# Four 64x64 tiles in place of a block-diagonal product for P V, a half batch in one step

## The chip, the cores and the metric

The kernel runs on one NeuronCore of one Trainium2 chip. The metric is the device time of one execution in microseconds (us); lower is better. The profiler records every instruction of TensorE (PE, with its weight loads as PEld), VectorE (DVE), ScalarE (ACT), GpSimd (POOL) and of the DMA queues.

## The reference

Linformer attention, then a gated feed-forward block. All inputs and the output are float32; the kernel works in bfloat16 with float32 accumulation.

```python
batch, n_heads, seq, head_dim, k_proj = 8, 8, 1024, 64, 64
k_proj = np.einsum('ks,bhsd->bhkd', E, k)
v_proj = np.einsum('ks,bhsd->bhkd', F, v)
scores = scale * np.matmul(q, k_proj.transpose(0, 1, 3, 2))
attn = softmax(scores)                       # over the 64 projected keys
attn_out = np.matmul(attn, v_proj)           # "P V": (1024 x 64) @ (64 x 64) for each head
x = attn_out.transpose(0, 2, 1, 3).reshape(8192, 512)
g = x @ w_gate; val = x @ w_val              # 512 -> 1536
return (g * sigmoid(g) * val) @ w_out        # 1536 -> 512
```

## The kernel before

**Chunks and steps.** A batch has two halves of 512 tokens; a half batch is a *chunk*, `c = 2*b + ch`, 0 to 15. The feed-forward block is the main loop: chunk `c` has 12 steps `f`, and a step `t = 12*c + f` computes one tile of 128 hidden features. `f_g` runs four 128x512 matmuls into a PSUM bank of pool `g` (two banks) and a tanh on ACT (line 474). `f_v` runs four more into a bank of pool `v` (two banks), and DVE joins them with two operations: line 481 (`s`, needs the tanh) and line 486 (`hT`, needs `s` and the `v` bank).

**Down projection.** Of chunk `c - 1`, it runs inside chunk `c`, from `late[t]`, right after `f_v` of its step. It is a seven-product scheme over two halves `p` of the token tiles: `f_m(c, n)`, `n` from 0 to 13, with `p, n % 7` choosing the product `m` in the order 3, 4, 5, 2, 1, 6, 7. A product is six 128x256 matmuls (line 564). Products 3, 4, 5, 2 of a half share the bank `y` (one bank); 1, 6, 7 share the bank `z` (one bank), and product 7 accumulates onto the columns that product 1 has filled. Between them, after product 6, `m_16` reads product 1 out of bank `z` on DVE (line 593), then adds on POOL (line 594). After product 7, `m_7` finishes on DVE (line 599) and the result is stored.

**Attention of later batches.** It is threaded through the main loop by slots: `slots[2*t]` runs between `f_g` and `f_v` of step `t`, and `slots[2*t + 1]` after `late[t]`. `place(b)` chooses the slots: the K and V projections (`u_KV`: 16 matmuls, 128x64 stationary, which write K to PSUM partitions 0 to 63 and V to 64 to 127 of one bank), scores and exp (`u_S`, eight a batch), row sums (`u_R` on DVE), normalisation (`u_N` on POOL), a transposing DMA (`u_AD`) that leaves the probabilities in `AT` with a pair of heads on the 128 partitions, and P V (`u_PV`).

**P V.** For a pair of heads, `BDV` holds the two projected 64x64 V matrices on the diagonal of a 128x128 tile, zeros elsewhere. One `u_PV` is one 128x512 matmul (line 410) into a bank of pool `a` (two banks), and one ACT copy (line 150) into `xT`, the input of the feed-forward block. A chunk needs four. In batches 3 to 7 the four of the first half are at slots 39, 41, 43, 45 from the batch's `s0 = 48*(b-1)`, which is after `f_v` of steps 7 to 10 of the odd chunk `2b - 1`; those of the second half at 57 to 63, steps 4 to 7 of the even chunk `2b`.

Nothing is reordered: every engine runs its instructions in the order in which this code issues them, and the banks come from rings (`bank`).

Of the kernel before, what the change touches and what calls it, by code (L numbers as in the profile page):

```python
# [18 lines left out]
D = 64  # L19
# [3 lines left out]
P = 128  # L23
# [15 lines left out]
def kernel(  # L39
# [38 lines left out]
    ident_bf = const.tile([P, P], BF16, name="ident_bf")  # L78
    ident_fp = fw.tile([P, P], FP32, name="ident_fp", tag="th")
    BD = [const.tile([P, H, P], BF16, name=f"BD{i}") for i in range(2)]  # L80
    BDV = [const.tile([P, NPAIR, P], BF16, name=f"BDV{i}") for i in range(2)]
    ks = [const.tile([P, H, D], BF16, name=f"ks{i}") for i in range(2)]
    ksp = [const.tile([P, NPAIR, D], BF16, name=f"ksp{i}") for i in range(2)]
    ET = const.tile([P, NJ, KP], BF16, name="ET")
# [67 lines left out]
    def u_KV(b, what="kv", hs=(0, H), at="a"):  # L152

        key = (b, what)
        if key not in kvp:
            kvp[key] = bank(at, [P, H, D], FP32, "kvp")
        t = kvp[key]
        h0, h1 = hs
        todo = [x for x in (("k", 0, ET, kb), ("v", 64, FT, vb)) if x[0] in what]
        for j in range(NJ):  # L160
            for _, lo, w, src in todo:
                nc.tensor.matmul(  # L162
                    out=t[lo : lo + 64, h0:h1].rearrange("p h d -> p (h d)"),
                    lhsT=w[:, j, :],
                    rhs=src[b][:, h0:h1, j, :],
                    start=(j == 0),
                    stop=(j == NJ - 1),
                )
        if "k" in what:
            nc.scalar.copy(out=ks[b % 2][0:64, h0:h1], in_=t[0:64, h0:h1])  # L170
        if "v" in what:
            tv = t[64:128].rearrange("p (a c) d -> p a c d", c=2)
            ps = slice(h0 // 2, h1 // 2)
            nc.vector.tensor_copy(out=BDV[b % 2][0:64, ps, 0:64], in_=tv[:, ps, 0, :])
            nc.vector.tensor_copy(out=BDV[b % 2][64:128, ps, 64:128], in_=tv[:, ps, 1, :])
        if h1 == H:
            kvp.pop(key)

# [15 lines left out]

    def u_V1(b, at="a"):

        t = bank(at, [P, NPAIR, D], FP32, "kvp")
        src = vb[b][:].rearrange("p (a c) j d -> p a c j d", c=2)
        for j in range(NJ):
            for c in range(2):  # L200
                nc.tensor.matmul(
                    out=t[64 * c : 64 * c + 64],
                    lhsT=FT[:, j, :],
                    rhs=src[:, :, c, j, :],
                    start=(j == 0),
                    stop=(j == NJ - 1),
                )
        for c in range(2):
            rows = slice(64 * c, 64 * c + 64)
            nc.vector.tensor_copy(out=BDV[b % 2][rows, :, rows], in_=t[rows])  # L210

    def u_V0(p0, p1, at):

        t = bank(at, [P, p1 - p0, P], FP32, "kvp")
        nc.tensor.matmul(
            out=t[:].rearrange("p a d -> p (a d)"),
            lhsT=zeros[:, 0:P], rhs=zeros[:, 0 : (p1 - p0) * P],
            start=True, stop=False,
        )
        src = vb[0][:].rearrange("p (a c) j d -> p a c j d", c=2)  # L220
        for j in range(NJ):
            for c in range(2):
                nc.tensor.matmul(
                    out=t[64 * c : 64 * c + 64, :, 64 * c : 64 * c + 64],
                    lhsT=FT[:, j, :],
                    rhs=src[:, p0:p1, c, j, :],
                    start=False,
                    stop=(j == NJ - 1),
                )
        nc.scalar.copy(out=BDV[0][:, p0:p1, :], in_=t[:])  # L230

    def u_V0w(p0, p1, at):

        t = bank(at, [P, p1 - p0, 2, D], FP32, "kvp")
        for j in range(NJ):
            nc.tensor.matmul(
                out=t[64:P].rearrange("p a c d -> p (a c) d"),
                lhsT=FT[:, j, :],
                rhs=vb[0][:, 2 * p0 : 2 * p1, j, :],
                start=(j == 0),  # L240
                stop=(j == NJ - 1),
            )
        for c in range(2):
            rows = slice(64 * c, 64 * c + 64)
            nc.scalar.copy(out=BDV[0][rows, p0:p1, rows], in_=t[64:P, :, c, :])

    def turn_ksp(t, b, g):
        nc.tensor.matmul(
# [95 lines left out]
    def u_S(b, u, at="a"):  # L344
        ch, w = divmod(u, 4)
        g, i = divmod(w, 2)
        ps = bank(at, [P, 4, P], FP32, "sc")
        if (b, ch) in BY_DMA:
            t = qT[b, ch, "d"][:].rearrange("p (h i) t -> p i h t", i=2)[:, i, 4 * g : 4 * g + 4]
        else:  # L350
            t = qT.pop((b, u))
        for n in range(4):
            nc.tensor.matmul(  # L353
                out=ps[:, n, :], lhsT=t[:, n, :], rhs=BD[b % 2][:, 4 * g + n, :], start=True, stop=True
            )
        e = aw.tile([P, 4, 2, KP], FP32, name="ee", tag="ee", bufs=4)
        nc.scalar.activation(  # L357
            out=e[:].rearrange("p h j k -> p (h j k)"),
            in_=ps[:].rearrange("p a k -> p (a k)"),
            func=AF.Exp,  # L360
            scale=scale,
        )
        ee[b, u] = e
# [42 lines left out]
    def u_PV(b, ch, pr, eng=nc.scalar):  # L406
        if (b, ch) not in xT:
            xT[b, ch] = x_pool.tile([P, NPAIR, CW], BF16, name="xT", tag=f"xT{ch}")
        ps = bank("a", [P, CW], FP32, "pv")
        nc.tensor.matmul(  # L410
            out=ps[:].rearrange("p (j t) -> p j t", t=P),
            lhsT=BDV[b % 2][:, pr, :],
            rhs=AT[b, ch][:, :, pr, :],
            start=True,
            stop=True,
        )
        copy(eng, xT[b, ch][:, pr, :], ps[:])

    def u_PV2(b, ch, g, i, eng):

        if (b, ch) not in xT:
            xT[b, ch] = x_pool.tile([P, NPAIR, CW], BF16, name="xT", tag=f"xT{ch}")
        ps = bank("a", [P, 2, CW // 2], FP32, "pv")
        for n in range(2):
            nc.tensor.matmul(
                out=ps[:, n].rearrange("p (j t) -> p j t", t=P),
                lhsT=BDV[b % 2][:, 2 * g + n, :],
                rhs=AT[b, ch][:, 2 * i : 2 * i + 2, 2 * g + n, :],
                start=True,
                stop=True,  # L430
            )
        copy(eng, xT[b, ch][:, 2 * g : 2 * g + 2, 256 * i : 256 * (i + 1)], ps[:])

    def u_PV1(b, ch, pr, i, eng):

        ps = bank("a", [P, CW // 2], FP32, "pv")
        nc.tensor.matmul(
            out=ps[:].rearrange("p (j t) -> p j t", t=P),
            lhsT=BDV[b % 2][:, pr, :],
            rhs=AT[b, ch][:, 2 * i : 2 * i + 2, pr, :],  # L440
            start=True,
            stop=True,
        )
        copy(eng, xT[b, ch][:, pr, 256 * i : 256 * (i + 1)], ps[:])
# [211 lines left out]
    def put(s, fn, *a):  # L656
        slots[s].append((fn, a))

    def place(b):
        s0 = 48 * (b - 1)  # L660
        if b == 1:
            put(22, u_TD, 1, 0)
            put(29, u_K1, 1)
            put(32, u_KT, 1)
            put(40, u_V1, 1)
            sa = (35, 36, 37, 38, 41, 42, 43, 44)
            put(41, u_AD, 1, 0)
            put(30, u_TD, 1, 1)
            put(47, u_AD, 1, 1)
            sp = (44, 45, 46, 46, 66, 67, 68, 69)  # L670
        else:
            put(s0 + (10 if b == 2 else 0), u_KV, b)
            put(s0 + (13 if b == 2 else 3), u_KT, b)
            o = 17 if b == 2 else 6
            put(s0 + (9 if b == 2 else -6), u_TD, b, 0)
            put(s0 + (11 if b == 2 else -4), u_TD, b, 1)
            sa = [s0 + o + 3 * j for j in range(NJ)]
            put(sa[3] + 4, u_AD, b, 0)
            put(sa[7] + 4, u_AD, b, 1)
            sp = [s0 + i for i in ((41, 43, 45, 46) if b == 2 else (39, 41, 43, 45)) + (57, 59, 61, 63)]  # L680
        for j in range(NJ):
            put(sa[j], u_S, b, j)
            put(sa[j] + 1, u_R, b, j)
            put(sa[j] + 1, u_N, b, j)
        for i in range(8):
            put(sp[i], u_PV, b, i // 4, i % 4)

    def run_slot(s):
        for fn, a in slots.pop(s, ()):
# [2 lines left out]
    with tc.manual_schedule():  # L692
# [17 lines left out]
        make_identity(nc, ident_fp[:])  # L710
        make_identity(nc, ident_bf[:])
        nc.vector.memset(ks[0][64:P], 0.0)
        nc.vector.memset(BDV[0][:, 0:2], 0.0)

        def turn(which, at, halves=(0, 1), eng=nc.scalar):
            for half in halves:
# [79 lines left out]
        f_mm(0, 1, 1, 0)  # L796
        nc.vector.memset(ks[1][64:P], 0.0)
        nc.vector.memset(BD[1][:], 0.0)
        nc.vector.memset(BDV[1][:], 0.0)
        load_w_gv(5, 7)  # L800
        load_w_gv(7, 8)
        load_q(0, 1, hs=(0, 4))
# [39 lines left out]
        for c in range(1, NC):  # L842
# [8 lines left out]
            else:  # L851
                for i, m in enumerate((1, 6, 7)):
                    late[(c + 1) * NFT + 1 + i].append((h_sum, c, m, 0, HF, nc.vector))
                for n, f in enumerate((0, 1, 2, 3, 4, 4, 5, 6, 7, 8, 9, 10, 10, 11)):
                    late[(c + 1) * NFT + f].append((f_m, c, n))

        for t in range(NIT):
# [40 lines left out]
```

## Time and profile before

| | |
|---|---|
| device time, three runs | 551.59, 551.61, 552.0 us; median 551.61 |
| the profiled execution | 551.3 us, of which the span is 549.5 us |
| granted TensorE clock, mean | 1.0 |
| busy: PE, DVE, ACT, POOL | 98%, 75%, 42%, 54% of the span |
| P V matmuls 128x512 (line 410) | 60, each 0.379 us from start to end (median) |
| copies of P V by ACT (line 150) | 63 with those of the first batch, median 0.585 us |
| V copies into `BDV` (lines 174, 175) | 12, each 0.43 us on DVE |

Durations of PE overlap, since matmuls are pipelined: what a matmul takes of PE is the distance to the start of the next one. The same holds, less strongly, for ACT and DVE.

### The profile page before, as it was taken

The page shows a single profiled execution, that of the slowest core. Times are in us where ns is not written, and L with a number is a line of the kernel's source. Part 1 is how long each engine was busy: PE and PEld are TensorE (multiplying, and loading weights), DVE is VectorE, ACT ScalarE, POOL GpSimd, SP SyncE. Part 2 cuts the span into 40 slices and gives each one's busy share as a digit, 9 for nine tenths or more (in the row PEclk, how much of TensorE's full clock was granted, in tenths as well). Part 3 has the DMA queues.
Part 4 walks back from the last instruction along what each step waited for, and adds up shares of the span by engine and source line. Part 5 has one row for each costly group of instructions (what it writes and reads, how often), then busy time and mean ns, then how long its engine had stood idle before and what let it go on. Part 6 is the DMA issues. An engine that isn't in the chain of part 4 may idle for free.

```text
span 549.5 us, 9272 instructions
## 1 busy us (share of the span) xinstructions
PE 536.9 (98%) x3438; PEld 317.4 (58%) x3500; DVE 414.5 (75%) x699; ACT 233.3 (42%) x416; POOL 294.6 (54%) x364
## 2 busy tenths in 40 slices
PE   7999999999999999999999999999999999999996
PEld 4654445566556555665555655566556565555565
DVE  3787897788597866978578785788859787676784
ACT  3664453444445433443435434344244533443331
POOL 6851494466627843386534855268461763526162
PEclk9999999999999999999999999999999999999999
DMA  9999989919963698029941399214990213110013
GB/s 205 192 197 188 162 150 178 179 39 140 197 124 78 116 197 149 10 69 159 195 106 39 76 163 197 66 39 93 178 211 18 72 46 76 39 40 17 23 39 116
DMA packets 111630, 62.87 MB, mean 114 GB/s; under 512 B 65888, under 2 KB 102752, under 8 KB 111584
## 3 DMA queue, kind: packets, MB, share of 16 engines
q0 software_dynamic: 43952, 29.49, 38.0%
q1 hardware_dynamic: 66800, 31.20, 26.4%
q10 hardware_dynamic: 832, 1.57, 0.9%
q8 instruction: 27, 0.44, 0.3%
q14 instruction: 19, 0.16, 0.1%
HBM read 60.29 MB, written 16.78 MB: 140 GB/s over the span
## 4 chain that ended last, share of the span: by engine, by line
PE 77%; DVE 10%; DMA 8%; issue 2%; POOL 2%; ACT 1%; DVEq 0%; POOLq 0%; ACTq 0%
PE gps L462 24%; PE vps L462 24%; PE yps L564 22%; DMA qTd<-qb 3%; DVE hs L547 2%; DVE s L481 2%; PE kvp L162 2%; DMA qb<-in_q_dram 2%; PE pv L410 2%; DVE hT L486 2%; PE sc L353 2%; DMA Fraw<-in_F_dram 1%; PE yps L498 1%; DMA wv<-in_moe_w_val_dram 1%; DVE BD L276 1%
## 5 line engine op out<-in xcount | busy, mean ns | idle before, releaser
L462 PE MATMUL vps<-xT,wv 128*128 128x512 bf16 (+1 forms) x761 | 195.0, 377 | 1.7 <-issue 0.8
L462 PE MATMUL gps<-xT,wg 128*128 128x512 bf16 (+1 forms) x727 | 191.0, 377 | 2.1
L474 ACT ACTIVATE th<-gps 128x512 f32<-128x512 f32 x191 | 114.1, 598 | 165.3 <-PE gps L462 149.4
L481 DVE SCALAR_TENSOR_TENSOR s<-th,gps 128x512 f32<-128x512 f32 x191 | 129.3, 677 | 66.3 <-ACT th L474 64.9
L547 POOL TENSOR_TENSOR hs<-hT 128x256 bf16<-128x256 bf16 x180 | 120.5, 691 | 58.9 <-DVE hT L486 58.1
L486 DVE SCALAR_TENSOR_TENSOR hT<-s,vps 128x512 bf16<-128x512 f32 x192 | 132.1, 688 | 20.4 <-PE gps L462 0.5
L462 PEld LDWEIGHTS <-wv 128*128 128x128 bf16 x776 | 73.8, 98 | 83.5 <-issue 3.0
L564 PEld LDWEIGHTS <-hs 128*128 128x128 bf16 x900 | 88.0, 98 | 35.7 <-issue 2.2
L462 PEld LDWEIGHTS <-wg 128*128 128x128 bf16 x776 | 73.9, 98 | 56.2 <-issue 0.6
L383 POOL TENSOR_TENSOR AAd<-ee,rr 128x512 bf16<-128x512 f32 x56 | 58.4, 1043 | 55.8 <-issue 33.7
L594 POOL TENSOR_TENSOR tt<-tt,ysb 128x512 f32<-128x512 f32 x28 | 35.5, 1267 | 68.2 <-DVE tt L593 68.2
L564 PE MATMUL yps<-ws,hs 128*128 128x256 bf16 x540 | 68.6, 272 | 0.4 <-DVE ysb L631 0.2
L583 POOL TENSOR_TENSOR tt<-xs 128x256 f32<-128x256 f32 x30 | 29.4, 982 | 52.2 <-ACT xs L581 52.1
L150 ACT CAST xT<-pv 128x512 bf16<-128x512 f32 (+1 forms) x63 | 36.4, 581 | 45.3 <-PE pv L410 44.2
L368 DVE TENSOR_REDUCE zz<-ee 128x8 f32<-128x512 f32 x64 | 43.3, 677 | 11.1 <-ACT ee L357 11.0
L564 PE MATMUL yps<-ws,hT 128*128 128x256 bf16 x360 | 48.8, 273 | 0.0
L564 PE MATMUL yps<-wo,hs 128*128 128x256 bf16 x360 | 48.6, 273 | 0.1
L547 DVE TENSOR_TENSOR hs<-hT 128x1536 bf16<-128x1536 bf16 (+1 forms) x49 | 46.1, 946 | 0.1
L357 ACT ACTIVATE ee<-sc 128x512 f32<-128x512 f32 x64 | 38.1, 598 | 18.2 <-PE sc L353 18.1
L564 PEld LDWEIGHTS <-hT 128*128 128x128 bf16 x360 | 35.2, 98 | 16.0
L581 ACT COPY xs<-yps 128x512 f32<-128x512 f32 x30 | 17.6, 585 | 30.4 <-PE yps L564 30.3
L588 ACT COPY ysb<-yps 128x512 f32<-128x512 f32 x30 | 17.6, 586 | 24.9 <-PE yps L564 21.6
(99 smaller groups left out, 318.0 us busy)
## 6 DMA issues: line engine op xcount, KB each, us to landing
out_dram<-ysb SPq DMA_DIRECT2D x28, 512.0 KB, 2.7
qb<-in_q_dram POOLq DMA_DIRECT2D x14, 512.0 KB, 19.2
kb<-in_k_dram POOLq DMA_DIRECT2D x7, 1024.0 KB, 10.0
vb<-in_v_dram POOLq DMA_DIRECT2D x7, 1024.0 KB, 14.8
wo<-in_moe_w_out_dram POOLq DMA_DIRECT2D x2, 768.0 KB, 21.5
out_dram<-ysb SPq DMA_DIRECT2D x6, 256.0 KB, 2.3
kraw<-in_k_dram ACTq DMA_DIRECT2D x2, 512.0 KB, 4.8
qb<-in_q_dram POOLq DMA_DIRECT2D x4, 256.0 KB, 7.8
```

Of the source, the lines that this page charges most:

```text
L150: (nc.scalar.copy if eng is nc.scalar else eng.tensor_copy)(out=out, in_=in_)
L357: nc.scalar.activation(out=e[:].rearrange("p h j k -> p (h j k)"), in_=ps[:].rearrange("p a k -> p (a k)"), func=AF.Exp, scale=scale,)
L368: nc.vector.reduce_sum(out=z[:], in_=e[:], axis=AX.X)
L383: eng.tensor_tensor(out=a.rearrange("p j h k -> p h j k"), in0=ee.pop((b, u))[:], in1=rr.pop((b, u))[:].unsqueeze(3).to_broadcast([P, 4, 2 ...
L462: nc.tensor.matmul(out=ps[:, ts], lhsT=(wg, wv)[w][:, kt, f * P : (f + 1) * P], rhs=x[:, kt, ts], start=(kt == 0), stop=(kt == NKT - 1),)
L474: nc.scalar.activation(out=th[:], in_=ps[:], func=AF.Tanh, scale=0.5)
L481: nc.vector.scalar_tensor_tensor(out=s1[:], in0=th[:], scalar=1.0, in1=g[:], op0=ALU.add, op1=ALU.mult)
L486: nc.vector.scalar_tensor_tensor(out=hT[c][:, f, :], in0=s1[:], scalar=0.5, in1=ps[:], op0=ALU.mult, op1=ALU.mult)
L547: eng.tensor_tensor(out=hs[c, m][:, fs, :], in0=quarter(hT[c], *a)[:, fs], in1=quarter(hT[c], *b)[:, fs], op=op,)
L564: nc.tensor.matmul(out=ps, lhsT=lhsT, rhs=ws[m][:, f, :] if rhs is None else rhs, start=(start and f == 0), stop=(f == HF - 1), skip_group ...
L583: nc.gpsimd.tensor_tensor(out=t[:, 0], in0=xs[:, 0], in1=xs[:, 1], op=ALU.add)
L594: nc.gpsimd.tensor_tensor(out=t[:], in0=t[:], in1=yo[c, p][:, 1:3], op=ALU.subtract)
```

## The change

For batches 1 to 7, the block-diagonal `BDV` is replaced by `VS`, which holds the 64x64 V matrices without zeros, heads `4g + 2r + e` on partitions `64r` to `64r + 63`. The scores of the heads are written in the order 0, 2, 1, 3, so that `AT` has the matching heads on its two halves of partitions. `u_PVt` does a chunk in one step: for each group `g` of four heads, four matmuls with a 64x64 stationary operand, two for the rows 0 to 63 and two for 64 to 127, each writing half the partitions of a bank; the row halves write separate banks. The second group takes the banks `y` and `z`. Then four ACT copies follow in a row, last bank first.

Where: the first half of a batch from 2 on at slot `s0 + 45` (after step 10 of chunk `2b - 1`), the second half of a batch from 1 on at `s0 + 69` (after step 10 of chunk `2b`). Batch 1's first half is two steps of one group each. Three score steps of a batch from 3 on come later (slots 24, 27, 30 in place of 21, 24, 27, with their row sums and the second transposing DMA), and one of batch 2 is a slot earlier. In the down projection `n` = 11, 12, 13 (products 1, 6, 7 of the second half) were at steps 10, 10, 11 and now all stand at step 11.

```diff
-    BDV = [const.tile([P, NPAIR, P], BF16, name=f"BDV{i}") for i in range(2)]
+    BDV = const.tile([P, NPAIR, P], BF16, name="BDV")
+    VS = [const.tile([P, 4, D], BF16, name=f"VS{i}") for i in range(2)]
...
+            tv = t[64:128].rearrange("p (g r e) d -> p g r e d", r=2, e=2)
+            for r in range(2):
+                vs = VS[b % 2][64 * r : 64 * r + 64].rearrange("p (g e) d -> p g e d", e=2)
+                nc.vector.tensor_copy(out=vs, in_=tv[:, :, r])
...
+            slot = (0, 2, 1, 3)[n] if (b, ch) in BY_DMA else n
...
+    def u_PVt(b, ch, gs, ats):
+        if (b, ch) not in xT:
+            xT[b, ch] = x_pool.tile([P, NPAIR, CW], BF16, name="xT", tag=f"xT{ch}")
+        todo = []
+        for g in gs:
+            ps = [bank(at, [P, CW], FP32, "pv") for at in ats[g]]
+            for r in range(2):
+                rows = slice(64 * r, 64 * r + 64)
+                for e in range(2):
+                    nc.tensor.matmul(
+                        out=ps[r][64 * e : 64 * e + 64].rearrange("p (j t) -> p j t", t=P),
+                        lhsT=VS[b % 2][rows, 2 * g + e, :],
+                        rhs=AT[b, ch][rows, :, 2 * g + e, :],
+                        start=True,
+                        stop=True,
+                    )
+            todo += [(2 * g + r, ps[r]) for r in range(2)]
+        for kt, ps in reversed(todo):
+            nc.scalar.copy(out=xT[b, ch][:, kt, :], in_=ps[:])
...
-            sp = (44, 45, 46, 46, 66, 67, 68, 69)
+            put(45, u_PVt, 1, 0, (0,), ("aa", "aa"))
+            put(46, u_PVt, 1, 0, (1,), ("aa", "aa"))
...
-            sa = [s0 + o + 3 * j for j in range(NJ)]
+            sa = [s0 + j for j in ((17, 19, 23, 26, 29, 32, 35, 38) if b == 2 else (6, 9, 12, 15, 18, 24, 27, 30))]
...
-            sp = [s0 + i for i in ((41, 43, 45, 46) if b == 2 else (39, 41, 43, 45)) + (57, 59, 61, 63)]
+            put(s0 + 45, u_PVt, b, 0, (0, 1), ("aa", "yz"))
...
-        for i in range(8):
-            put(sp[i], u_PV, b, i // 4, i % 4)
+        put(s0 + 69, u_PVt, b, 1, (0, 1), ("aa", "yz"))
...
-                for n, f in enumerate((0, 1, 2, 3, 4, 4, 5, 6, 7, 8, 9, 10, 10, 11)):
+                for n, f in enumerate((0, 1, 2, 3, 4, 4, 5, 6, 7, 8, 9, 11, 11, 11)):
                     late[(c + 1) * NFT + f].append((f_m, c, n))
```

More of the change, by code (lines that the diff above doesn't have):

```diff
@@ L171, in u_KV @@
         if "v" in what:
[L172 to L175, printed above, removed]
+            tv = t[64:128].rearrange("p (g r e) d -> p g r e d", r=2, e=2)
+            for r in range(2):
+                vs = VS[b % 2][64 * r : 64 * r + 64].rearrange("p (g e) d -> p g e d", e=2)
+                nc.vector.tensor_copy(out=vs, in_=tv[:, :, r])
         if h1 == H:
@@ L195, in u_V1 @@
     def u_V1(b, at="a"):
-        t = bank(at, [P, NPAIR, D], FP32, "kvp")
-        src = vb[b][:].rearrange("p (a c) j d -> p a c j d", c=2)
+        t = bank(at, [P, 4, D], FP32, "kvp")
+        src = vb[b][:].rearrange("p (g r e) j d -> p g r e j d", r=2, e=2)
         for j in range(NJ):
-            for c in range(2):
+            for r in range(2):
                 nc.tensor.matmul(
-                    out=t[64 * c : 64 * c + 64],
+                    out=t[64 * r : 64 * r + 64].rearrange("p (g e) d -> p g e d", e=2),
                     lhsT=FT[:, j, :],
-                    rhs=src[:, :, c, j, :],
+                    rhs=src[:, :, r, :, j, :],
                     start=(j == 0),
@@ L207, in u_V1 @@
                 )
-        for c in range(2):
-            rows = slice(64 * c, 64 * c + 64)
-            nc.vector.tensor_copy(out=BDV[b % 2][rows, :, rows], in_=t[rows])
+        nc.vector.tensor_copy(out=VS[b % 2][:], in_=t[:])
     def u_V0(p0, p1, at):
@@ L229, in u_V0 @@
                 )
-        nc.scalar.copy(out=BDV[0][:, p0:p1, :], in_=t[:])
+        nc.scalar.copy(out=BDV[:, p0:p1, :], in_=t[:])
     def u_V0w(p0, p1, at):
@@ L244, in u_V0w @@
             rows = slice(64 * c, 64 * c + 64)
-            nc.scalar.copy(out=BDV[0][rows, p0:p1, rows], in_=t[64:P, :, c, :])
+            nc.scalar.copy(out=BDV[rows, p0:p1, rows], in_=t[64:P, :, c, :])
     def turn_ksp(t, b, g):
@@ L352, in u_S @@
         for n in range(4):
+            slot = (0, 2, 1, 3)[n] if (b, ch) in BY_DMA else n
             nc.tensor.matmul(
-                out=ps[:, n, :], lhsT=t[:, n, :], rhs=BD[b % 2][:, 4 * g + n, :], start=True, stop=True
+                out=ps[:, slot, :], lhsT=t[:, n, :], rhs=BD[b % 2][:, 4 * g + n, :], start=True, stop=True
             )
@@ L411, in u_PV @@
             out=ps[:].rearrange("p (j t) -> p j t", t=P),
-            lhsT=BDV[b % 2][:, pr, :],
+            lhsT=BDV[:, pr, :],
             rhs=AT[b, ch][:, :, pr, :],
@@ L417, in u_PV @@
         copy(eng, xT[b, ch][:, pr, :], ps[:])
+    def u_PVt(b, ch, gs, ats):
[4 more added lines that the diff above has]
+            ps = [bank(at, [P, CW], FP32, "pv") for at in ats[g]]
+            for r in range(2):
+                rows = slice(64 * r, 64 * r + 64)
[10 more added lines that the diff above has]
+            nc.scalar.copy(out=xT[b, ch][:, kt, :], in_=ps[:])
     def u_PV2(b, ch, g, i, eng):
@@ L426, in u_PV2 @@
                 out=ps[:, n].rearrange("p (j t) -> p j t", t=P),
-                lhsT=BDV[b % 2][:, 2 * g + n, :],
+                lhsT=BDV[:, 2 * g + n, :],
                 rhs=AT[b, ch][:, 2 * i : 2 * i + 2, 2 * g + n, :],
@@ L438, in u_PV1 @@
             out=ps[:].rearrange("p (j t) -> p j t", t=P),
-            lhsT=BDV[b % 2][:, pr, :],
+            lhsT=BDV[:, pr, :],
             rhs=AT[b, ch][:, 2 * i : 2 * i + 2, pr, :],
@@ L673, in place @@
             put(s0 + (13 if b == 2 else 3), u_KT, b)
-            o = 17 if b == 2 else 6
             put(s0 + (9 if b == 2 else -6), u_TD, b, 0)
             put(s0 + (11 if b == 2 else -4), u_TD, b, 1)
-            sa = [s0 + o + 3 * j for j in range(NJ)]
+            sa = [s0 + j for j in ((17, 19, 23, 26, 29, 32, 35, 38) if b == 2 else (6, 9, 12, 15, 18, 24, 27, 30))]
             put(sa[3] + 4, u_AD, b, 0)
             put(sa[7] + 4, u_AD, b, 1)
-            sp = [s0 + i for i in ((41, 43, 45, 46) if b == 2 else (39, 41, 43, 45)) + (57, 59, 61, 63)]
+            put(s0 + 45, u_PVt, b, 0, (0, 1), ("aa", "yz"))
         for j in range(NJ):
@@ L712 @@
         nc.vector.memset(ks[0][64:P], 0.0)
-        nc.vector.memset(BDV[0][:, 0:2], 0.0)
+        nc.vector.memset(BDV[:, 0:2], 0.0)
         def turn(which, at, halves=(0, 1), eng=nc.scalar):
@@ L798 @@
         nc.vector.memset(BD[1][:], 0.0)
-        nc.vector.memset(BDV[1][:], 0.0)
         load_w_gv(5, 7)
```

## The prediction

> **What bounds the kernel now.** I read the page first, then who PE waited for, then the order in time on PE, ACT and DVE around the end of a chunk.
>
> ```profile
> PE 536.9 (98%) x3438; PEld 317.4 (58%) x3500; DVE 414.5 (75%) x699; ACT 233.3 (42%) x416; POOL 294.6 (54%) x364
> ```
>
> PE is busy for 98%. The list of PE's waits names 3.4 us of waits for data in the whole span, all but 0.2 in the first 18 us; between there and the tail the only recorded gaps are five of 0.16 us behind K and V projections. So PE has no slack in its main loop: a matmul less is a gain at full price, and a new wait on PE is a loss at full price.
>
> The order in time on PE, end of chunk 7 and start of chunk 8 (columns: start, length, engine, line, operation, tiles, shape, count):
>
> ```profile
> 274.00 1.47 PE L564 MATMUL yps<-ws,hs 128*128 128x256 bf16 x12
> 275.31 0.38 PE L410 MATMUL pv<-AT,BDV 128*128 128x512 bf16 x1
> 275.53 1.03 PE L462 MATMUL gps<-xT,wg 128*128 128x512 bf16 x4
> 276.39 1.03 PE L462 MATMUL vps<-xT,wv 128*128 128x512 bf16 x4
> 277.26 0.82 PE L564 MATMUL yps<-ws,hs 128*128 128x256 bf16 x6
> 277.91 1.03 PE L462 MATMUL gps<-xT,wg 128*128 128x512 bf16 x4
> 278.87 0.40 PE L162 MATMUL kvp<-kb,ET 128*64 128x512 bf16 x1
> 278.87 0.40 PE L162 MATMUL kvp<-vb,FT 128*64 128x512 bf16 x1
> 279.11 0.38 PE L162 MATMUL kvp<-kb,ET 128*64 128x512 bf16 x1
> ...
> 280.41 0.38 PE L162 MATMUL kvp<-vb,FT 128*64 128x512 bf16 x1
> 280.94 0.81 PE L462 MATMUL vps<-xT,wv 128*128 128x512 bf16 x3 [0.16 <-issue]
> ```
>
> Prices from starts: a 128x512 matmul takes 0.216 us (four from 275.53 to 276.39), a product of six 0.655 (half of 274.00 to 275.31); an end lies 0.16 behind its slot (0.38 less 0.216). The K and V pairs, two column halves of the array with different moving data, start together: 0.216 a pair. Entering that mode costs 0.10 (278.77 due, 278.87 seen) and 0.02 in the first pair; leaving costs 0.10 (280.62 due; one of the four records is missing, so the first began at 280.94 less 0.216).
>
> ACT, with four operations queued, and a tanh that had nothing before it:
>
> ```profile
> 235.90 0.58 ACT L581 COPY xs<-yps 128x512 f32<-128x512 f32 x1 [0.98 <-PE yps L564]
> 236.38 0.59 ACT L150 CAST xT<-pv 128x512 bf16<-128x512 f32 x1
> 236.86 0.62 ACT L357 ACTIVATE ee<-sc 128x512 f32<-128x512 f32 x1
> 237.35 0.62 ACT L474 ACTIVATE th<-gps 128x512 f32<-128x512 f32 x1
> ...
> 276.59 0.60 ACT L474 ACTIVATE th<-gps 128x512 f32<-128x512 f32 x1 [0.28 <-PE gps L462]
> ```
>
> Back to back, ACT takes 0.48 us an operation, whatever it is; it starts 0.04 us behind the end of its matmul (276.55, 276.59).
>
> DVE at steps 4 (first two lines), 10 and 11:
>
> ```profile
> 259.68 0.69 DVE L486 SCALAR_TENSOR_TENSOR hT<-s,vps 128x512 bf16<-128x512 f32 x1
> 260.28 0.41 DVE L593 TENSOR_TENSOR tt<-tt,yps 128x256 f32<-128x256 f32 x1
> ...
> 274.76 0.69 DVE L486 SCALAR_TENSOR_TENSOR hT<-s,vps 128x512 bf16<-128x512 f32 x1
> 275.58 0.42 DVE L593 TENSOR_TENSOR tt<-tt,yps 128x256 f32<-128x256 f32 x1
> 277.22 0.69 DVE L481 SCALAR_TENSOR_TENSOR s<-th,gps 128x512 f32<-128x512 f32 x1 [1.22 <-ACT th L474]
> 278.01 0.69 DVE L486 SCALAR_TENSOR_TENSOR hT<-s,vps 128x512 bf16<-128x512 f32 x1
> 278.62 0.68 DVE L599 TENSOR_TENSOR ysb<-tt,yps 128x512 f32<-128x512 f32 x1
> ```
>
> Tanh to `s` takes 0.63, `s` to `hT` 0.79, `hT` to the next operation 0.60. The line to watch is L593, `m_16`: it reads product 1 out of bank `z`, and product 7, which adds onto the same columns, may not start before. Now the two are a step apart: L593 ends at 276.00, product 7 starts at 277.26, 1.26 us later, so the wait costs nothing.
>
> **The change, part by part.** Time 0 is the end of `f_v` of step 10 on PE (274.00 above).
>
> *P V on PE, chunks 2 to 14 (13 steps).* Removed: 4 x 0.216 = 0.86 us. Added: eight 64x64 matmuls. No row shows two row halves at once. If all four of a group share a slot as the column pairs do, it is 2 x 0.216 = 0.43, plus the mode change, 0.22: 0.65, a gain of 0.21. If only column pairs share, 0.86 + 0.22: a loss of 0.22. One after another, 8 x 0.216 + 0.22: a loss of 1.09. I take 0.21, since the pairs, the nearest row, start within 0.01 us of each other. The Trainium skill (TensorEngine Tiling (Array Packing), Tiling Modes, Key Properties) says that a change of the tiling mode drains the TensorE. The trace agrees that it costs, 0.10 each way; without that drain the gain would be 0.43. Chunk 1 has two steps of one group: 2 x 0.44 against 0.86, nothing.
>
> *Product 7 behind `m_16`.* Products 1, 6, 7 are now adjacent on PE at step 11, and in the changed instruction order L593 stands on DVE behind `s` and `hT` of step 11, those wait for the tanh of step 11, and on ACT that tanh stands behind the four copies. On PE product 7 carries the wait, and all of chunk `c + 1` is queued behind it. Chain: P V takes its slots from 0.10 to 0.56; its end is seen at 0.72, the first copy starts at 0.76 (ACT idle: the tanh of step 10 is over at -0.06). Four copies at 0.48: the tanh starts at 2.69, where its data were there at 1.73. `s` 3.32, `hT` 4.11, L593 4.71, its end 5.13, product 7 at 5.18 (0.05 from a DVE end to PE, as at 543.62 to 543.67 in the tail). PE alone: mode left at 0.66, `f_g` and `f_v` to 2.39, products 1 and 6 to 3.70. Wait: 1.48 us a chunk. Ends: copies at their full 0.59 each give 1.48 + 0.44 = 1.92; no delay by the copies leaves the chain from product 6 itself: L593 starts 0.27 behind its slot (275.58 against 275.31), takes 0.42, then 0.05: 0.74. The Trainium skill (same page, PSUM Bottleneck) says that tiling does not speed up the copies out of PSUM, which may become the bottleneck, and advises to share them between ScalarE and VectorE. The trace agrees: 1.93 us of copies against 0.65 of P V; with two of the four on DVE the wait would fall to about the 0.74 above, an estimate from these rows, and the sum by 13 x 0.74 = 9.6 us.
>
> *Chunk 15* has the moved products but no P V: 0.74 once.
>
> *Nothing:* `VS` is filled by two DVE copies like `BDV` (one for batch 1, one memset less), off PE's path. The reversed copies free `z` and `y` first (`z` by 1.4, product 1 needs it at 2.39). `xT` is complete by 3.2, PE reads it at 5.8. The moved scores put one more row sum and reciprocal (0.83) before L593 of step 4 in chunks 5 to 13: 260.28 becomes 261.11, end 261.53; product 7 there starts at 261.45, plus 0.22 for the score matmuls that moved in. It just fits; if that cover goes, 0.3 x 5 = 1.5. POOL's add (1.27) ends at 6.6, before DVE needs its place for step 0 (7.5). The transposing DMAs have more time than before, so SP's queue gets no new wait.
>
> Sum: 13 x (1.48 - 0.21) + 0.74 = 17.3 us. The profiled execution is 551.3 (span 549.5 and 1.8 around it), 0.3 under the median of the runs; 551.6 + 17.3 = 568.9.
>
> **Rivals.**
> *Faster: PE gains and product 7 does not wait.* For it: 0.21 x 13 = 2.7 us, so 548.9 (546.0 if the modes cost nothing). It decides if L593 ends before 3.65, that is if copies, tanh, `s`, `hT` and L593 took 1.5 us less than their rows; even with no copies the 0.74 is left. Against: every link is in the order of the program and has a row. 0.05.
> *Slower by less: the copies do not delay the tanh*, only the adjacency counts. 13 x (0.74 - 0.21) + 0.74 = 7.6: 559.2. For it: ACT is 42% busy. Against: its copies stand ahead in an in-order queue. 0.12.
> *Tiles share nothing across rows.* 13 x (1.48 + 0.22) + 0.74 and chunk 1's 0.44: 23.3, 574.9; quite serial, 13 x (1.48 + 1.09) + 0.74 + 1.3: 35.5, 587. Against: the column pairs. 0.13, mostly the first.
> *The change does little:* gain and waits cancel, wait about 0.2. 0.02.
>
> **How the numbers follow.** The forecast, 568.9, has 0.68: with the copies' upper price it is 574.6, with a wait 0.4 shorter 563.7. The range adds the milder and the pairs-only cases: 558 to 577. A measurement can tell about 0.2% (1.1 us). Faster takes the first rival and a little for an unseen gain, 0.06; same 0.02; slower 0.92.
>
> **What would show it.** In the changed trace: four P V matmuls starting together, twice, a mode gap of 0.10; four copies 0.48 apart and the tanh behind them; before product 7 of step 11 a PE wait of about 1.5 us put down to DVE L593 in chunks 2 to 14, 13 times, and about 0.7 in chunk 15; PE's share of busy time down to some 94%. No such wait, or P V groups of 0.43 us and more, would make it wrong.

## The result and the profile after

| | before | after |
|---|---|---|
| device time, median of 6 runs | 551.68 us | 570.91 us (570.68 to 571.61) |
| the profiled execution, span | 551.3, 549.5 | 570.83, 569.1 |
| PE busy, mean granted clock | 98%, 1.0 | 95%, 1.0 |

The ratio is 1.0349, with a 95% interval of 1.0335 to 1.0362: 19.2 us slower. The forecast was 568.9 with a range of 558 to 577.

The page of the changed kernel, and its list of PE's waits (waiting and waited for, us in total, times, longest):

```profile
PE 541.6 (95%) x3556; PEld 312.9 (55%) x3556; DVE 413.4 (73%) x697; ACT 231.0 (41%) x416; POOL 295.0 (52%) x364
```
```profile
PE yps L586 <- DVE tt L615: 19.6, 19, 1.4
```

PE's busy time is 4.7 us higher than before (541.6 against 536.9), though the P V steps take less of it. At each wait the recorded end of the last matmul, 0.16 us behind its slot, counts as busy, 3.0 us for 19 waits; the rest was not traced. What is new is that PE stands still 19 times for one DVE line. L615 is `m_16`, which was L593 before: the read of product 1 out of bank `z`. That line was not in the list of before at all.

The order in time on PE, end of chunk 7 (steps 10 and 11), which answers to the stretch at 274.00 of before:

```profile
280.07 1.03 PE L484 MATMUL vps<-xT,wv 128*128 128x512 bf16 x4
281.02 0.63 PE L430 MATMUL pv<-AT,VS 64*64 64x512 bf16 x8
281.58 1.04 PE L484 MATMUL gps<-xT,wg 128*128 128x512 bf16 x4
282.45 1.03 PE L484 MATMUL vps<-xT,wv 128*128 128x512 bf16 x4
283.32 1.47 PE L586 MATMUL yps<-ws,hs 128*128 128x256 bf16 x12
286.15 0.81 PE L586 MATMUL yps<-ws,hs 128*128 128x256 bf16 x6 [1.36 <-DVE tt L615]
```

The slot of a matmul is the time from its start to the next one's when nothing waits, 0.216 us for 128x512. `f_v` of step 10 ends its slots at 280.93, `f_g` of step 11 starts at 281.58: the whole P V step, mode changes included, takes 0.65 us. Products 1 and 6 are due to end at 283.32 + 1.31 = 284.63; product 7 starts at 286.15. Counted from start to start that is a wait of 1.52 us; the recorded gap, 1.36, is 0.16 shorter because it starts at the end of the last matmul in the pipe.

What it waits for, on ACT and then on DVE:

```profile
281.70 2.05 ACT L439 CAST xT<-pv 128x512 bf16<-128x512 f32 x4 [0.84 <-PE pv L430]
283.62 0.64 ACT L496 ACTIVATE th<-gps 128x512 f32<-128x512 f32 x1
```
```profile
284.29 0.69 DVE L503 SCALAR_TENSOR_TENSOR s<-th,gps 128x512 f32<-128x512 f32 x1 [1.91 <-ACT th L496]
285.08 0.69 DVE L508 SCALAR_TENSOR_TENSOR hT<-s,vps 128x512 bf16<-128x512 f32 x1
285.68 0.41 DVE L615 TENSOR_TENSOR tt<-tt,yps 128x256 f32<-128x256 f32 x1
```

Four copies, then the tanh of step 11 at 283.62 without an idle moment ahead of it (its data were there at about 282.65), then `s`, `hT`, the read, which ends at 286.09, and product 7 at 286.15.

### The profile page after: what moved, and what is told of

Read it like the earlier page. It is cut to its first block, busy times and chain, and to the rows that moved or that the text cites. A ratio compares the mean times of both kernels' runs of the same rounds, so it can differ in the third digit from the quotient of the medians.

```text
span 569.1 us, 9443 instructions
## 1 busy us (share of the span) xinstructions
PE 541.6 (95%) x3556; PEld 312.9 (55%) x3556; DVE 413.4 (73%) x697; ACT 231.0 (41%) x416; POOL 295.0 (52%) x364
## 5 line engine op out<-in xcount | busy, mean ns | idle before, releaser
L484 PE MATMUL vps<-xT,wv 128*128 128x512 bf16 (+1 forms) x776 | 197.5, 377 | 0.0
L484 PE MATMUL gps<-xT,wg 128*128 128x512 bf16 (+1 forms) x772 | 196.7, 377 | 0.3 <-DMA wg<-in_moe_w_gate_dram 0.3
L586 PE MATMUL yps<-ws,hs 128*128 128x256 bf16 x540 | 68.5, 272 | 19.7 <-DVE tt L615 19.6
L357 ACT ACTIVATE ee<-sc 128x512 f32<-128x512 f32 x64 | 37.9, 596 | 19.8 <-PE sc L353 19.7
L621 DVE TENSOR_TENSOR ysb<-tt,yps 128x512 f32<-128x512 f32 x28 | 19.2, 685 | 20.2 <-POOL tt L616 20.2
L439 ACT CAST xT<-pv 128x512 bf16<-128x512 f32 x56 | 28.8, 598 | 12.1 <-PE pv L430 12.1
## 6 DMA issues: line engine op xcount, KB each, us to landing
kb<-in_k_dram POOLq DMA_DIRECT2D x7, 1024.0 KB, 10.8
```

The lines of the kernel that those rows point to most:

```text
L357: nc.scalar.activation(out=e[:].rearrange("p h j k -> p (h j k)"), in_=ps[:].rearrange("p a k -> p (a k)"), func=AF.Exp, scale=scale,)
L439: nc.scalar.copy(out=xT[b, ch][:, kt, :], in_=ps[:])
L484: nc.tensor.matmul(out=ps[:, ts], lhsT=(wg, wv)[w][:, kt, f * P : (f + 1) * P], rhs=x[:, kt, ts], start=(kt == 0), stop=(kt == NKT - 1),)
L586: nc.tensor.matmul(out=ps, lhsT=lhsT, rhs=ws[m][:, f, :] if rhs is None else rhs, start=(start and f == 0), stop=(f == HF - 1), skip_group ...
```

## The experiments

The lines that time a wait below are read from starts, as above: start of product 7 less the end of the slots before it.

### The adjacency alone

On the kernel before:

```diff
-                for n, f in enumerate((0, 1, 2, 3, 4, 4, 5, 6, 7, 8, 9, 10, 10, 11)):
+                for n, f in enumerate((0, 1, 2, 3, 4, 4, 5, 6, 7, 8, 9, 11, 11, 11)):
```

> The kernel before with one edit: products 1, 6, 7 of the second half all at step 11 (P V stays block-diagonal, spread over the steps). Theory (product 7 waits for the DVE read of product 1, which stands behind s and hT of step 11): without the train of four copies the wait is 0.74 us in each of chunks 2 to 15, 14 x 0.74 = 10.4, so about 562.0 us; PE waits put down to the DVE line of that read, about 0.6 us each as recorded gaps. Rival (only the four copies cost, the adjacency is free): 551.7 us.

Measured: 562.3 us against 551.73, ratio 1.019 (1.0173 to 1.0207). PE, then DVE, of that kernel at the end of chunk 7:

```profile
280.03 1.47 PE L564 MATMUL yps<-ws,hs 128*128 128x256 bf16 x12
282.08 0.82 PE L564 MATMUL yps<-ws,hs 128*128 128x256 bf16 x6 [0.58 <-DVE tt L593]
```
```profile
280.79 0.69 DVE L486 SCALAR_TENSOR_TENSOR hT<-s,vps 128x512 bf16<-128x512 f32 x1
281.61 0.42 DVE L593 TENSOR_TENSOR tt<-tt,yps 128x256 f32<-128x256 f32 x1
```

Product 7 is due at 280.03 + 1.31 = 281.34 and starts at 282.08: 0.74. In the even chunks from 4 to 12 the wait is 0.81 or 0.82, since a row sum and a reciprocal stand ahead of `s` on DVE there; in the nine others it is 0.74 or 0.75; together 10.8. So more than half of the loss comes from a row of numbers in a list, without P V having been touched: with products 1, 6, 7 side by side, product 7 waits for a DVE read that here begins 0.27 us behind the slots of product 6 (281.61 against 281.34). The read takes only product 1's half of the bank, but the program issues it after product 6. No run issues it between the two, so whether that would save most of this wait is open.

### Half of the copies on DVE

On the changed kernel:

```diff
-            nc.scalar.copy(out=xT[b, ch][:, kt, :], in_=ps[:])
+            copy(nc.scalar if kt >= 2 or len(todo) == 2 else nc.vector, xT[b, ch][:, kt, :], ps[:])
```

> The changed kernel with two of the four copies of a step (banks of pool a) on DVE instead of ACT. Theory: the tanh of step 11 comes 0.97 us earlier, the wait before product 7 falls from 1.52 us to the 0.74 us of the adjacency itself, 13 x 0.78 = 10.1 us less than 570.9: about 560.8 us. Rival 1 (the copies are not what delays the read): 570.9 us. Rival 2 (the two copies on DVE stand in front of s and hT of step 11 and delay the read as much as they did on ACT): about 566 us or more.

Measured: 560.82 us, ratio to before 1.0162 (1.0147 to 1.0177), 10.1 below the change. ACT, DVE and PE of that kernel, end of chunk 7:

```profile
278.13 1.07 ACT L151 CAST xT<-pv 128x512 bf16<-128x512 f32 x2 [0.84 <-PE pv L430]
279.09 0.61 ACT L496 ACTIVATE th<-gps 128x512 f32<-128x512 f32 x1
```
```profile
278.72 1.28 DVE L151 CAST xT<-pv 128x512 bf16<-128x512 f32 x2
279.92 0.68 DVE L503 SCALAR_TENSOR_TENSOR s<-th,gps 128x512 f32<-128x512 f32 x1
```
```profile
281.81 0.81 PE L586 MATMUL yps<-ws,hs 128*128 128x256 bf16 x6 [0.58 <-DVE tt L615]
```

The tanh comes right behind two copies, the wait is back at the 0.58 (0.75 by starts) of the adjacency. DVE does pay: `s` waits for its copies from about 279.72 to 279.92, but the read is then still bound by product 6. In chunks 2 and 8 DVE pays more, and the waits there are 0.90 and 1.09. The copies of a train on one engine were the other half of the loss: 10.1 us by the medians, where the estimate from the rows was 9.6. In the profiled executions the waits at step 11 shrink by 9.6 us (20.6 to 10.9), and another 0.6 us goes behind PE's last matmuls, so that the match with the 10.1 that was expected is in part luck. More could not be had, since the adjacency stays. To share the copies between the two engines is what the Trainium skill advises (TensorEngine Tiling (Array Packing), PSUM Bottleneck); the trace agrees, with these 9.6 us.

### The read ahead of the feed-forward of its step

On the changed kernel, products 1 and 6 between `f_g` and `f_v` of step 11:

```diff
-                    late[(c + 1) * NFT + f].append((f_m, c, n))
+                    if n in (11, 12):
+                        put(2 * ((c + 1) * NFT + f), f_m, c, n)
+                    else:
+                        late[(c + 1) * NFT + f].append((f_m, c, n))
```

> The changed kernel with products 1 and 6 (and the DVE read after them) between f_g and f_v of step 11, product 7 still after f_v: the read stands ahead of s and hT of step 11 on DVE, and f_v (0.86 us) lies between product 6 and product 7, more than the 0.74 us that the read needs. Theory: all waits at step 11 go, chunks 2 to 14 keep the gain of 0.21 us each from P V: 551.7 - 2.7, plus the 0.21 us of wait that came up at step 4 of six even chunks (1.3): about 550.3 us. Rival (the P V step, its tiling mode or the copies cost PE something beyond that wait): above 553 us.

Measured: 550.75 us, ratio 0.9984 (0.9975 to 0.9993). PE and DVE, end of chunk 7:

```profile
275.04 1.47 PE L586 MATMUL yps<-ws,hs 128*128 128x256 bf16 x12
276.35 1.03 PE L484 MATMUL vps<-xT,wv 128*128 128x512 bf16 x4
277.22 0.82 PE L586 MATMUL yps<-ws,hs 128*128 128x256 bf16 x6
```
```profile
276.62 0.42 DVE L615 TENSOR_TENSOR tt<-tt,yps 128x256 f32<-128x256 f32 x1 [1.66 <-PE yps L586]
276.96 0.68 DVE L503 SCALAR_TENSOR_TENSOR s<-th,gps 128x512 f32<-128x512 f32 x1
```

The read is over at 277.04, product 7 starts at 277.22 on time, in every chunk. The four copies are still in a row on ACT and cost nothing here. 20.2 us between this kernel and the change: the whole loss, and a little more, hung on the place of two products and of the read that follows them.

### Packing taken back

The kernel above, with the block-diagonal `BDV` and four 128x128 matmuls in the step, all else (place, banks, copies) as it is; the filling of `BDV` and the order of the scores go back with it, and the cut shows the matmuls alone:

```diff
-                for e in range(2):
-                    nc.tensor.matmul(
-                        out=ps[r][64 * e : 64 * e + 64].rearrange("p (j t) -> p j t", t=P),
-                        lhsT=VS[b % 2][rows, 2 * g + e, :],
-                        rhs=AT[b, ch][rows, :, 2 * g + e, :],
+                nc.tensor.matmul(
+                    out=ps[r][:].rearrange("p (j t) -> p j t", t=P),
+                    lhsT=BDV[b % 2][:, 2 * g + r, :],
+                    rhs=AT[b, ch][:, :, 2 * g + r, :],
```

> As the run with products 1 and 6 between f_g and f_v, but P V by four block-diagonal 128x512 matmuls in the same step, banks and copies: packing alone taken back. Theory: 13 x 0.21 = 2.7 us above that run, about 553.0 us (step of 0.86 us against 0.65). Rival 1 (row halves of the array do not share a slot, so that packing is worth nothing or costs): equal to that run or up to 3 us below it. Rival 2 (the mode change costs nothing): 13 x 0.43 = 5.6 us above it.

Measured: 553.69 us, ratio to before 1.0036 (1.0023 to 1.0049), 2.9 above the kernel with packing. PE there, then with packing:

```profile
274.51 1.03 PE L429 MATMUL pv<-AT,BDV 128*128 128x512 bf16 x4
275.37 1.03 PE L483 MATMUL gps<-xT,wg 128*128 128x512 bf16 x4
```
```profile
273.61 0.63 PE L430 MATMUL pv<-AT,VS 64*64 64x512 bf16 x8
274.17 1.04 PE L484 MATMUL gps<-xT,wg 128*128 128x512 bf16 x4
```

0.86 us against 0.56 from the first start, to which 0.09 of entering the mode belongs (`f_v` ended at 273.52): 0.65. So the four tiles of a group do share one slot, and the mode change takes half of what they save. The rival of row halves that do not share is out, and so is that of a free mode change (5.6 us). These step lengths are a cleaner measure than the 2.9 us: the profiled execution without packing also has a wait of 0.54 us for a DMA and one of 0.57 in chunk 9 that the other lacks, and lacks its wait of 0.42 in chunk 4.

### Product 7 of the first half, a step later

Starts on PE of before show a wait that the list of waits leaves out, in five even chunks. In chunk 8 of before and of the change, `f_v` of step 5 and product 7 of the first half:

```profile
294.07 1.03 PE L462 MATMUL vps<-xT,wv 128*128 128x512 bf16 x4
295.15 0.82 PE L564 MATMUL yps<-ws,hs 128*128 128x256 bf16 x6
```
```profile
302.75 1.03 PE L484 MATMUL vps<-xT,wv 128*128 128x512 bf16 x4
304.04 0.81 PE L586 MATMUL yps<-ws,hs 128*128 128x256 bf16 x6 [0.27 <-DVE tt L615]
```

Four matmuls take 0.86: before, product 7 is 295.15 - 294.93 = 0.22 late, after, 304.04 - 303.61 = 0.43. The read of step 4 is late there in both, because DVE works without a break in steps 0 to 4 behind the K and V projection. Before and after:

```profile
294.68 0.41 DVE L593 TENSOR_TENSOR tt<-tt,yps 128x256 f32<-128x256 f32 x1
303.57 0.41 DVE L615 TENSOR_TENSOR tt<-tt,yps 128x256 f32<-128x256 f32 x1
```

It ends at 295.09 and 303.98, right ahead of product 7. Before, the P V matmul at step 4 (292.77) filled 0.216 of that time; the change moved it away.

Two runs move product 7 (`n` = 6) from step 5 to step 6, on the kernel before and on the one with the read ahead:

```diff
-                for n, f in enumerate((0, 1, 2, 3, 4, 4, 5, 6, 7, 8, 9, 10, 10, 11)):
+                for n, f in enumerate((0, 1, 2, 3, 4, 4, 6, 6, 7, 8, 9, 10, 10, 11)):
```

> The kernel before with product 7 of the first half (n = 6) at step 6 instead of 5. Counted from starts of matmuls, the kernel before waits 0.21 us ahead of that product in five even chunks (4, 6, 8, 10, 12), too short to show as a recorded gap. Theory (the read of product 1 at step 4 is late there because DVE is full in steps 0 to 4 behind the K and V projection): the five waits go, 5 x 0.21 = 1.05 us, about 550.7 us. Rival (that stretch is bound by DVE as a whole, so the wait only moves to the next step): 551.7 us.

Measured: 550.97 us (551.62 for before beside it), ratio 0.9983 (0.9974 to 0.9992). 0.65 won of 1.05 by the medians, 0.9 by the ratio; the interval, 0.4 to 1.4 us, holds the theory's value and leaves out the rival's zero. The five waits at step 5 are gone from the trace. In the profiled execution PE waits 0.46 ahead of one score step of batch 2 instead; what that does to the median was not followed.

> The kernel with products 1 and 6 between f_g and f_v of step 11, and in addition product 7 of the first half at step 6 instead of 5. Theory (the wait there grew from 0.21 to 0.43 us because the P V matmul of 0.216 us that stood at step 4 of the even chunks moved to step 10): five waits of 0.43 go, 2.15 us under 550.75: about 548.6 us, with no PE wait of over 0.1 us left between 95 us and the tail. Rival (DVE-bound stretch, the wait moves on): 550.5 us and more.

Measured: 548.69 us, ratio 0.9947 (0.9934 to 0.9959), 2.1 below the same kernel without the move, as expected. Between 95 us and the tail the list of PE's waits names none for DVE. This version beats both kernels, by 2.9 and 22.2 us.

### The old places, and other banks

The changed kernel with the list of before; P V's second group in `y` and a bank of `g`:

```diff
-            put(s0 + 45, u_PVt, b, 0, (0, 1), ("aa", "yz"))
+            put(s0 + 45, u_PVt, b, 0, (0, 1), ("aa", "yg"))
...
-        put(s0 + 69, u_PVt, b, 1, (0, 1), ("aa", "yz"))
+        put(s0 + 69, u_PVt, b, 1, (0, 1), ("aa", "yg"))
...
-                for n, f in enumerate((0, 1, 2, 3, 4, 4, 5, 6, 7, 8, 9, 11, 11, 11)):
+                for n, f in enumerate((0, 1, 2, 3, 4, 4, 5, 6, 7, 8, 9, 10, 10, 11)):
```

> The changed kernel with products 1, 6, 7 of the second half back at steps 10, 10, 11, and the second group of P V in banks y and g (z is in use). Four copies in a row on ACT, tiles and step as in the change. Theory: the read of product 1 is over before the copies start, no wait at step 11; 13 x 0.21 gained, 5 x 0.21 lost at step 4: about 550.3 us, as with products 1 and 6 early. Rival (the copies in a row delay the feed-forward itself: the tanh of step 11 late, or f_g waiting for the lent bank): PE waits at step 11 or step 0 and 552 us or more.

Measured: 553.57 us, ratio 1.0038 (1.0025 to 1.0051): 3.3 above what my theory said. There is no wait at step 11, but a new one ahead of product 7 at step 5 of the odd chunks, 0.3 to 0.96 us, 3.1 in all. ACT and DVE of that kernel, end of chunk 6, and PE at step 5 of chunk 7:

```profile
244.88 2.06 ACT L439 CAST xT<-pv 128x512 bf16<-128x512 f32 x4 [2.15 <-PE pv L430]
246.80 0.64 ACT L496 ACTIVATE th<-gps 128x512 f32<-128x512 f32 x1
```
```profile
247.47 0.69 DVE L503 SCALAR_TENSOR_TENSOR s<-th,gps 128x512 f32<-128x512 f32 x1 [2.67 <-ACT th L496]
248.62 0.69 DVE L508 SCALAR_TENSOR_TENSOR hT<-s,vps 128x512 bf16<-128x512 f32 x1 [0.46 <-PE sc L353]
249.22 0.68 DVE L621 TENSOR_TENSOR ysb<-tt,yps 128x512 f32<-128x512 f32 x1
249.82 0.68 DVE L503 SCALAR_TENSOR_TENSOR s<-th,gps 128x512 f32<-128x512 f32 x1
```
```profile
263.07 0.82 PE L586 MATMUL yps<-ws,hs 128*128 128x256 bf16 x6 [0.79 <-DVE tt L615]
```

Here step 11 is short on PE (one product instead of three), so the tanh that the copies have pushed to 246.80 is not made up for within the step: from 248.62 DVE runs without a gap, and 14 us later its read of step 4 ends so late that product 7 starts 0.96 us behind its turn. But the copies are only part of that lag. Of the two lines below the first is from this kernel and the second from the one with the read ahead:

```profile
253.38 1.51 DVE L569 TENSOR_TENSOR hs<-hT 128x1536 bf16<-128x1536 bf16 x1
252.34 0.95 DVE L569 TENSOR_TENSOR hs<-hT 128x1536 bf16<-128x1536 bf16 x1
```

Counted from `f_g` of step 0 (247.16 and 246.65), this operation of DVE starts 0.53 us later here, and it takes 0.56 longer, in all five of these odd chunks; the read of step 4 then comes 1.10 later, where 0.15 was to spare. What lengthens the operation was not followed. So the push of the copies accounts for at most about half of that lag, and no run at these places takes it apart. To see whether only that read turns the lag into time, the same kernel with `n` = 6 at step 6:

> The kernel with the second half's products 1, 6, 7 at their old places and P V in banks y and g (553.57 us), and product 7 of the first half at step 6 instead of 5. Its trace has waits of 0.43 us in five even chunks and 0.3 to 0.96 us (3.1 in all) in five odd chunks, all ahead of that product: the copies in a row push the tanh of step 11 back and DVE carries the lag into steps 0 to 4. Theory (only that read of step 4 turns the lag into a PE wait): both sets go, 2.15 + 3.1 less, about 548.3 us. Rival (the lag is DVE's bound for the stretch and shows at another place): 551 us or more.

Measured: 549.62 us (548.36 to 550.01), ratio 0.9953 (0.9939 to 0.9966): 3.95 won of the 5.25 expected. All ten waits are gone. The profiled execution has one of another kind, 1.28 us of PE by starts (1.12 as recorded) for a transposing DMA of q ahead of the first scores of batch 2 (the DMA is issued at 152.29, in the kernel before at 150.70); it is as large as the 1.30 that are missing. The five times of this kernel spread over 1.65 us, so how often that wait comes is open.

## Why the prediction was right, point by point

| term | predicted | measured |
|---|---|---|
| P V on PE, 13 steps | -0.21 each, -2.7 | 0.65 a step, -2.7; 2.9 by the run without packing |
| wait before product 7, chunks 2 to 14 | 1.48 each, 19.2 | 1.52 each, 19.8 |
| chunk 15, adjacency alone | 0.74 | 0.74 |
| first half's product 7, step 5 | 0 (odd chunks 0 to 1.5) | 5 x 0.21 = 1.1, in even chunks |
| chunk 1, two steps of one group | 0 | 0.3 |
| sum | 17.3 | 19.2 (medians: 19.2) |

The chain of the main term held link by link: copies to tanh 1.92 us (1.93 said), tanh to `s` 0.67 (0.63), `s` to `hT` 0.79, `hT` to the read 0.60, the read 0.41, to PE 0.06. Its two halves were shown apart: the adjacency by itself costs 0.74 us a chunk (10.6 us when put alone into the kernel before), and the copies the rest (10.1 us when two of the four are taken from ACT). The adjacency is enough by itself to slow the kernel down. Its 0.74 us is the way from product 6 over the read to product 7, with nothing on PE to fill it; the copies come on top because of the order of ACT's and DVE's instructions. With the read moved ahead on DVE and `f_v` put between product 6 and product 7, both vanish together; that run does not tell the two apart. With the products at their old places the copies cost nothing at step 11, and at most a part of 3.1 us at another product 7.

The term that was missed at step 5 is small, and the mistake behind it is worth naming. I took the five gaps of 0.16 us among the recorded idle times as proof that PE waits nowhere else. A wait under about 0.16 us past a matmul's slot does not show there at all, and one of 0.22 shows as 0.05. With starts instead of gaps, the stretch of steps 0 to 4 in even chunks is seen to be bound by DVE already, so that P V matmuls taken out of it are not won. I had looked for the danger in the odd chunks, where one more row sum moved in: there the read just fits, as forecast, until something else makes DVE late, as in the run with the old places.

A second term was put at nothing and is not: chunk 1, two steps of one group, 2 x 0.44 against 0.86. Its two steps in the changed kernel:

```profile
77.40 0.41 PE L430 MATMUL pv<-AT,VS 64*64 64x512 bf16 x4
78.71 0.70 PE L430 MATMUL pv<-AT,VS 64*64 64x512 bf16 x4
```

The first takes 0.44 us, as forecast. The second takes 0.74 (78.61 to 79.35), because its last matmul starts at about 79.0 instead of with the others. ACT is at work on the copies of the first step until 78.96, which fits a wait for a bank; the run without packing has a delay at the same place (0.25), but no run tests it.

The profiled executions differ by a little more than the medians, 19.6 us of span; 0.25 of that is there by 74 us, where PE's list has small waits for a weight transfer (0.3) and for POOL (0.2). I did not follow them. The errors all go one way: 0.04 us in each of 13 waits, 1.1 at step 5 and 0.3 in chunk 1, so that no error hides another.

Of the rivals, "the copies do not delay the tanh" is refuted by the half of the copies on DVE, "tiles share nothing across rows" by the run without packing, and "product 7 does not wait" is what a kernel with the read ahead shows: it would have been right at another place of two products, with 550.75 against the 548.9 that it was given.

## What to carry to other kernels

When PE has no slack, ask of every moved accumulation who must read the bank between two of its parts, and what stands ahead of that reader in its own queue: the price of a move is the whole queue, here a train of copies, a tanh and two DVE operations, for a gain of 0.21 us. Put independent matmuls between the last write and the next, and issue the read ahead of the step's own work, as the run with the read ahead does. And measure waits on a pipelined engine from start to start; the recorded gaps here leave out the first 0.16 us of each.

## What the runs showed of the hardware

The prediction could only assume this from the column pairs: four 64x64 tiles of one group, two row halves and two column halves, with different moving data and two banks, share one slot of 0.216 us: eight matmuls take 0.55 or 0.56 us from the first start to the next instruction in all 13 steps, of which two slots are 0.43. Entering that mode costs 0.09 us (280.93 to 281.02) and leaving it about 0.1, as for the two column halves of the K and V projection; the block-diagonal step has no gap ahead of it (273.65 + 0.86 = 274.51). So half of the gain of a step of two groups goes into the change of mode.
